# A planned three-stage kernel whose order now comes from backward plans, with stores of y and of hi parts issued by ScalarE

## The chip, the cores and the metric

The kernel runs on one core of a Trainium2 chip, in one launch. The metric is device time in microseconds (us), the median of several runs. The engines are named as in the profile: PE is TensorE's matmul unit and PEld its weight load, DVE is VectorE, ACT is ScalarE, POOL is GpSimd, SP is SyncE, which here does nothing but issue transfers.

## What is computed

```python
def sm_attn(qq, kk, vv):
    s = scale * np.matmul(qq, kk.transpose(0, 1, 3, 2))
    s = s - np.max(s, axis=-1, keepdims=True)
    a = np.exp(s)
    a = a / (np.sum(a, axis=-1, keepdims=True) + 1e-09)
    return np.matmul(a, vv)
p_packed = sm_attn(p, k, v)               # 8 batches, 8 heads, 576 tokens, 32 packed, 64 wide
out = sm_attn(q, p_packed, p_packed)
...
h = x @ w_in                              # x: out as 4608 tokens x 512; w_in: 512 x 1024
sm = softmax(h); solu = h * sm
ln = (solu - mean(solu)) / sqrt(var(solu) + 1e-06) * g_ln
x = ln @ w_out                            # 1024 x 512
...
g = relu(x @ moe2_w_in) ** 2              # 512 x 2048
return g @ moe2_w_out                     # 2048 x 512
```

The weights come as 64-bit floats, which the kernel turns into 32-bit ones itself. Data is 32-bit; most products are made as three products of hi and lo parts (hi*hi, hi*lo, lo*hi).

## The kernel before

The program has three stages that flow into each other. In the first, 16 units (a batch and four of its heads) are packed (`pack`: scores `s1`, their exponentials `e1`, transposes `pt`, the product `ppp` with the rows of v, and its transpose `ptp`, which becomes `ppq`) and unpacked (`unpack`: scores `s2` of q, a softmax over the 32 packed rows, its transposition to `aT`, and the product `pg` of the packed rows with w_in, kept as `G`). A group of 128 tokens (`h_tile`) makes h as `ph` from `G` and the split parts `ah`, `al` of `aT`, goes through softmax and layer norm to `e`, and is transposed (`ptv`) and split into `v`. For 256 tokens `y_stage` makes y = v times w_out in four banks `py` of 24 products each; ACT copies a bank to `ysb`, and a transfer stores it to `y_dram`. Beside it, 16 pieces of moe2's first matrix are decoded from 64-bit floats (`prepare`), summed for a Strassen-like scheme of 7 products, split into hi (`wh`) and lo (`wx`) and stored to `z_dram`. The second stage (`z_group`, tiles `px`, `pw`, `pz` from `y` and `zi`) makes g and stores it to `g_dram`; 16 pieces of moe2's second matrix are prepared beside it and stored to `o_dram`. The third (`o_products`, tiles `px`, `pa` from `oi` and `cb`) makes the output from g, which is loaded as `ga` and split into `cb`.

Nothing is written in the order in which it runs. Each piece of work is handed to a planner as an operation of one engine (`Plan.op`) or of one of several (`Plan.either`), with an estimated duration, the buffers that it reads and writes, and an **urgency**: a number in us, made by hand-set constants (`att_at`, `T0`, `DT`, `PD`, `WD`, `YB` and others). `Plan.order` (line 148) plays the operations forward through its own estimates; whenever an engine is free it takes the able operation of the lowest urgency, and a shared buffer goes to the lowest urgency that asks for it. The sequence in which operations start is the program's order: each engine, and each queue of transfers, runs its own operations in that order and waits at the head for what the head needs. All transfers of before but 18 of the last output stores are issued by SP (line 373, `dma`), so a store whose data is late holds the loads behind it.

```python
def dma(at, out_, in_, nbytes, r=(), w=(), spare=0, queue=nc.sync):
    plan.op(DMA, max(430.0, nbytes / 358.0), at, lambda: queue.dma_start(out=out_(), in_=in_()), r=r, w=w, lag=2200 + spare)
```

Eight PSUM banks serve PE: in the first stage four of them (`bank`, one shared ring) take turns for `s1`, `pt`, `ppp`, `ptp`, `s2`, `pg`, `ptv` and `py`, and two `ph` tiles hold two each. The lines that matter below: 404 to 406 (the three products of `mm`), 386 and 389 (hi and lo of a split), 478 and 560 (scores), 648 (`pg`), 696 and 719 (`ph`), 762 (`ptv`), 785 (`ysb`), 438 (the last addition of a decoded weight), 733 and 750 (passes over `e`).

Of the kernel before, what the change touches and what calls it, by code (L numbers as in the profile page):

```python
# [9 lines left out]
F32 = mybir.dt.float32  # L10
# [9 lines left out]
PE, ACT, DVE, POOL, DMA = range(5)  # L20
# [70 lines left out]
class Plan:  # L91

    WINDOW = 3413.0

# [22 lines left out]
    def either(self, engines, urgency, fn, r=(), w=(), lag=0, claim=(), port=False):  # L120
# [25 lines left out]
        self.ops.append(Op(engines, urgency, fn, lag, bufs, deps, port))  # L146

    def order(self):
        ops = self.ops
        users = [[] for _ in ops]  # L150
# [29 lines left out]
        order = []  # L180
# [11 lines left out]
        def take(e, t):  # L192
            nonlocal port
            while not busy[e] and able[e]:
                _, i = heapq.heappop(able[e])
                o = ops[i]
                if o.engine is not None:
                    continue
                o.engine = e
                busy[e] = True  # L200
                order.append(i)
                if e == POOL or e == DVE and o.port:
                    port = self.span = max(t, port) + o.engines[e]
                else:
                    self.span = pe_end(t, o.engines[e]) if e == PE else t + o.engines[e]
                heapq.heappush(events, (self.span, i, "free"))
# [29 lines left out]

    def emit(self):
        with self.tc.manual_schedule():
            for i in self.order():
# [6 lines left out]
def kernel(  # L246
# [25 lines left out]
    nc = tc.nc  # L272
# [5 lines left out]
    P = 128  # L278
# [4 lines left out]
    KJ = (S + P - 1) // P  # L283
    SH = S // 2
    ST = 256
    AB, GB, RAW, TMP, VR, ET = 4, 4, 1, 2, 1, 1
    QA, GA, HA, TR, UN = 55.91, 149.84, 34.68, -39.93, -11.33
    NK = 4
    WD, WDS, WIS = 99.51, 175.52, 17.0
    GSC = (POOL,)  # L290
    SIN, SOUT = DVE, ACT
    GX = 1
    SUB, KLO, ALO = (POOL,), (DVE,), (DVE,)
    ZSIN, OSIN = DVE, DVE
    SN, FN, LATE = 5.72, -26.79, 3090.0
    YB, ZL, OL, GL0, GL1, GL2, PS, CS = 197.3, 148.71, 20.73, 15.29, 13.31, 32.6, 1.04, 186.23
    NST = NT // ST
# [39 lines left out]
    y_dram = [dram.tile([P, CD, 2 * HN], F32, name=f"y_dram{i}", tag=f"y{i}") for i in range(NSZ)]  # L337
# [32 lines left out]

    def dma(at, out_, in_, nbytes, r=(), w=(), spare=0, queue=nc.sync):

        plan.op(DMA, max(430.0, nbytes / 358.0), at, lambda: queue.dma_start(out=out_(), in_=in_()), r=r, w=w, lag=2200 + spare)
# [98 lines left out]
    pbz = [ab.tile([P, 2, HG, 32] if i == 0 else [P, 2, 2, 32], F32, f"pbz{i}") for i in range(3)]  # L472
    PAIR = 4 * (0.4336 * SH + 6)

# [17 lines left out]
    def pack(at, b, g):  # L492
# [105 lines left out]
        def pp_mm():  # L598
            for j in range(KJ):
                m = rows[j]  # L600
                for e in range(2):
                    nc.tensor.matmul(
                        ppp()[64 * e:64 * e + 64, :2 * D].rearrange("p (h m i) -> p h m i", h=2, m=2),
                        eT()[:m, j, 64 * e:64 * e + 64], vr()[:m, 2 * e:2 * e + 2, j, :].rearrange("p m (h i) -> p h m i", h=2), start=j == 0, stop=j == KJ - 1)
        plan.op(PE, KJ * 267, at + 10, pp_mm, r=[eT, vr], w=[ppp])

# [20 lines left out]
    def unpack(at, b, g, packed):  # L627
# [13 lines left out]
        for f in range(F1 // 512):  # L641
            pg = bank("pg")
            fs = slice(f * 512, (f + 1) * 512)

            def g_mm(pg=pg, fs=fs):
                for e in range(2):
                    es = slice(64 * e, 64 * e + 64)
                    nc.tensor.matmul(pg()[es, :], ppq()[:, e], wi[2 * g + e]()[:, fs], start=True, stop=True)  # L648
            plan.op(PE, 885, at + GA, g_mm, r=[ppq, wi[2 * g], wi[2 * g + 1]], w=[pg], claim=[gt])
            hi_op(at + GA + 1, 512, lambda fs=fs: gt()[:, 0, fs], pg, [pg], [gt])  # L650
            if b >= GX:
                lo_op(at + GA + 1, 512, lambda fs=fs: gt()[:, 1, fs], pg, lambda fs=fs: gt()[:, 0, fs], [pg, gt], [gt], (DVE,))
# [116 lines left out]
    def y_stage(at, st):  # L769
        vh, vl = v_tiles.pop(st)  # L770
        t, o = divmod(st * ST, 2 * HN)
        for d in range(CD):
# [8 lines left out]
            for half in range(2):  # L781
# [4 lines left out]
                    r=[py], w=[ysb] + [under_way] * (st == d == 0))  # L786
            dma(at - YB, lambda d=d: y_dram[t][:, d, o:o + ST], ysb, P * ST * 4, r=[ysb], w=[ydep[t]])

# [5 lines left out]
    def prepare(at, w_bits, rows2, cols2, outs, marks, tiles, sign, r=(), engines=BOTH, spare=0):  # L794
# [11 lines left out]
        lo_op(at, 7 * P, lambda: x().bitcast(F32R), x, hi, [hi], [x], engines)  # L806
        dma(at, outs[0], lambda: hi().bitcast(F32), P * 7 * P * 4, r=[hi], w=marks)
        dma(at, outs[1], x, P * 7 * P * 4, r=[x], w=marks)
# [7 lines left out]

    T0, DT = 127.57, 23.948
    PD0, PD = 111.2, 23.139
    UD, UA, U1 = 25.541, 213.28, -45.68
    WI, WO, WOD, YL = 162.35, 266.68, 65.988, 3.36  # L820
    units = [(b, g) for b in range(B) for g in range(NG)]
# [31 lines left out]
    ORDER = (1, 2, 6, 5, 7, 3, 4)  # L853
    DZ, DO = 5.018, 7.511
    T1 = T0 + DT * NT / P
# [302 lines left out]
    second()  # L1158
    plan.emit()

# [29 lines left out]
```

## Time and profile before

| what | value |
|---|---|
| median of 3 runs (lowest, highest) | 1265.01 us (1264.72, 1267.79) |
| the profiled execution | 1262.49 us, of which 1260.4 us are its span |
| PE busy | 1205.5 us, 96% of the span, 8332 products |
| DVE, ACT, POOL busy | 906.0, 789.7, 171.7 us |
| mean granted TensorE clock | 0.985 |
| transfers | 234.60 MB, mean 186 GB/s |

How to read it: busy PE is time in which at least one product is under way, and the ends of products are modelled, so the span between two starts tells more than a duration. The span starts with the first instruction and ends with the last; the execution's own time has 2.1 us around it.

### The profile page before, as it was taken

The numbers are of one execution on the slowest core, as the hardware profiler recorded it, in microseconds if no ns is written. First come the engines' busy times: TensorE is split into PE (matmuls) and PEld (weight loads), VectorE is DVE, ScalarE is ACT, GpSimd is POOL, SyncE is SP. The second block draws the span as 40 slices with busy tenths as digits, with TensorE's granted clock in tenths as the row PEclk, the third lists the DMA queues.
The fourth block names the chain that finished last, engine by engine and source line by source line (L and its number), as shares of the span: only waits on it lengthen the run. The fifth ranks groups of instructions, "written<-read, shape, count | busy, mean of one in ns | idle before, by whom it ended". The sixth has DMA issues, their size and how long they took to land.

```text
span 1260.4 us, 23326 instructions
## 1 busy us (share of the span) xinstructions
PE 1205.5 (96%) x8332; PEld 1101.2 (87%) x8332; DVE 906.0 (72%) x1817; ACT 789.7 (63%) x1678; POOL 171.7 (14%) x181
## 2 busy tenths in 40 slices
PE   4668999999999999999999999999899999999998
PEld 2336788877888789999999999999899999999998
DVE  5888678787766874455686868662678787878786
ACT  2476577666776666577777878777554555555453
POOL 1364323333332340000000000000000000000000
PEclk9878999999999999999999999999899999999999
DMA  8856756776756649465767676753986535343501
GB/s 214 224 154 168 204 156 174 216 197 170 205 150 193 171 125 329 157 200 197 242 199 248 205 249 206 230 166 130 351 341 210 157 121 158 112 151 110 171 32 51
DMA packets 185240, 234.60 MB, mean 186 GB/s; under 512 B 24356, under 2 KB 148772, under 8 KB 184356
## 3 DMA queue, kind: packets, MB, share of 16 engines
q1 hardware_dynamic: 184260, 232.33, 60.2%
q8 instruction: 65, 1.06, 0.4%
q10 hardware_dynamic: 864, 0.79, 0.2%
q14 instruction: 51, 0.42, 0.1%
HBM read 130.55 MB, written 85.98 MB: 172 GB/s over the span
## 4 chain that ended last, share of the span: by engine, by line
PE 78%; DMA 5%; DVE 4%; ACT 3%; issue 1%; SPq 1%; ACTq 0%; DVEq 0%
PE px L404 9%; PE px L406 8%; PE px L405 8%; PE ph L719 7%; PE py L404 5%; PE py L405 5%; PE py L406 5%; PE pa L404 5%; PE pa L406 5%; PE pa L405 5%; PE ptv L762 3%; PE s L478 2%; PE pg L648 2%; PE pz L406 2%; PE pz L405 2%; PE pz L404 2%
## 5 line engine op out<-in xcount | busy, mean ns | idle before, releaser
L386 ACT CAST cb<-ga 128x384 fp32r<-128x384 f32 x336 | 168.0, 513 | 168.3 <-PE px L406 70.9
L389 DVE TENSOR_TENSOR cb<-ga,cb 128x384 fp32r<-128x384 f32 x336 | 180.5, 555 | 60.8 <-ACT cb L386 59.5
L404 PE MATMUL py<-v,wo 128*128 128x256 f32 x576 | 169.3, 294 | 0.0
L405 PE MATMUL py<-v,wo 128*128 128x256 f32 x576 | 163.5, 284 | 0.0
L406 PE MATMUL py<-v,wo 128*128 128x256 f32 x576 | 163.2, 283 | 0.0
L404 PE MATMUL px<-oi,cb 128*128 128x256 f32 x504 | 142.8, 283 | 2.9 <-ACT cb L386 2.9
L406 PE MATMUL px<-oi,cb 128*128 128x256 f32 x504 | 142.5, 283 | 0.8 <-DVE cb L389 0.8
L405 PE MATMUL px<-oi,cb 128*128 128x256 f32 x504 | 142.4, 282 | 0.0
L404 PE MATMUL pa<-oi,cb 128*128 128x256 f32 x504 | 141.4, 281 | 0.0
L406 PE MATMUL pa<-oi,cb 128*128 128x256 f32 x504 | 141.0, 280 | 0.0
L405 PE MATMUL pa<-oi,cb 128*128 128x256 f32 x504 | 141.0, 280 | 0.0
L404 PE MATMUL px<-y,zi 128*128 128x384 f32 x384 | 130.3, 339 | 1.8 <-ACT gw L963 1.7
L405 PE MATMUL px<-y,zi 128*128 128x384 f32 x384 | 129.6, 337 | 0.4 <-DVE y L389 0.3
L406 PE MATMUL px<-y,zi 128*128 128x384 f32 x384 | 129.3, 337 | 0.0
L404 PEld LDWEIGHTS py<-v,wo 128*128 128x128 f32 x576 | 110.6, 192 | 9.1 <-issue 7.8
L967 DVE TENSOR_TENSOR gw<-pz,gw 128x384 f32<-128x384 f32 x96 | 53.2, 554 | 81.1 <-PE pz L406 66.2
L405 PEld LDWEIGHTS py<-v,wo 128*128 128x128 f32 x576 | 110.8, 192 | 0.7
L406 PEld LDWEIGHTS py<-v,wo 128*128 128x128 f32 x576 | 110.6, 192 | 0.0
L907 DVE TENSOR_TENSOR ga<-ga 128x384 f32<-128x384 f32 x192 | 99.7, 552 | 2.6 <-DMA ga<-g_dram 1.9
L404 PEld LDWEIGHTS px<-oi,cb 128*128 128x128 f32 x504 | 96.4, 191 | 3.2 <-ACT cb L386 3.2
L406 PEld LDWEIGHTS px<-oi,cb 128*128 128x128 f32 x504 | 96.5, 191 | 1.1 <-DVE cb L389 1.1
L975 ACT ACTIVATE gw<-gw 128x384 f32<-128x384 f32 x115 | 60.2, 523 | 57.5 <-DVE gw L967 57.1
(180 smaller groups left out, 2990.8 us busy)
## 6 DMA issues: line engine op xcount, KB each, us to landing
g_dram<-gw SPq DMA_DIRECT2D x192, 192.0 KB
ga<-g_dram SPq DMA_DIRECT2D x96, 384.0 KB
zi<-z_dram SPq DMA_DIRECT2D x28, 512.0 KB
oi<-o_dram SPq DMA_DIRECT2D x24, 512.0 KB
kr<-in_k_dram SPq DMA_DIRECT2D x16, 576.0 KB
qr<-in_q_dram SPq DMA_DIRECT2D x16, 576.0 KB
q<-qT SPq DMA_DIRECT2D x64, 144.0 KB
y_dram<-ysb SPq DMA_DIRECT2D x72, 128.0 KB
```

What stands on the lines that cost most here:

```text
L386: plan.op(ACT, c_act(cols, sbuf=r[0].pool not in (psm, psh, pso)), at, lambda: nc.scalar.copy(out_(), in_()), r=r, w=w)
L389: plan.either(on(cols, *engines), at, lambda e: vec[e].tensor_tensor(out_(), in_(), hi_().bitcast(F32), op=ALU.subtract), r=r, w=w, port=i ...
L404: nc.tensor.matmul(ps, lh, rh, start=first, stop=False, skip_group_check=onto)
L405: nc.tensor.matmul(ps, lh, rl, start=False, stop=False, skip_group_check=onto)
L406: nc.tensor.matmul(ps, ll, rh, start=False, stop=last, skip_group_check=onto)
L478: nc.tensor.matmul(ps()[64 * e:64 * e + 64, :SH], cols(lhs, e), cols(rhs, e)[:, cs], start=True, stop=True)
L648: nc.tensor.matmul(pg()[es, :], ppq()[:, e], wi[2 * g + e]()[:, fs], start=True, stop=True)
L719: nc.tensor.matmul(ph()[:, fs], al[l]()[:, g], g_tiles[b, g]()[:, r, fs], start=ends[0] and g == 0 and t == 0, stop=ends[1] and g == NG - ...
L762: nc.tensor.transpose(pt()[:, c * P:(c + 1) * P], e()[:, (4 * t + c) * P:(4 * t + c + 1) * P], ident)
L907: plan.op(DVE, c_dve(cols), at, lambda: nc.vector.tensor_tensor(out_(), in0(), in1(), op=op), r=r, w=w, port=True)
L967: plan.op(DVE, c_dve(HN), when(p, SN), lambda: nc.vector.tensor_tensor(t(), ps()[:, :HN], t(), op=ALU.add), r=[t, ps], w=[t])
L975: nc.scalar.activation(t(), t(), AF.Relu)
```

## The change

Three things are changed. First, the order is no longer planned once. `emit` plans forward as before, then eight times (`PASSES`) plans the same operations backward from the end, with the engines and buffer slots that the forward plan chose, and takes each operation's distance from the end of the backward plan as its new urgency before it plans forward again. The hand-set constants only feed the first plan; several have new values. Second, the planner's estimates differ: every transfer lands 1500 ns later (`spare=1500` by default), and `s1`/`s2`, `ppp` and `pg` last a little longer. Third, 72 stores of y, 16 of `z_dram`'s hi part and 16 of `o_dram`'s hi part are issued from ACT's queue (`queue=nc.scalar`), and the subtraction that makes `al` belongs to POOL instead of DVE (`ALO`). No product is added or removed: PE has the same 7962 instructions in another order. Lines of the changed kernel carry numbers 65 higher.

```diff
+    def reset(self):
+        for o in self.ops:
+            o.engine = None
+            for b in o.bufs:
+                b.slot = None
+                if b.ring:
+                    b.ring.free, b.ring.queue = list(range(b.ring.bufs)), []
+
+    def backward(self):
+
+        ops, ends = self.ops, self.ends
+        deps = [set(o.deps) for o in ops]
+        slots = {}
+        for b in dict.fromkeys(b for o in ops for b in o.bufs if b.slot is not None):
+            slots.setdefault((b.ring, b.slot), []).append(b)
+        for bufs in slots.values():
+            bufs.sort(key=lambda b: ends[b.touched[0]])
+            for a, b in zip(bufs, bufs[1:]):
+                deps[b.touched[0]].update(a.touched)
...
+                for j in sorted(deps[i]):
+                    left[j] -= 1
+                    free[j] = max(free[j], t + self.hop(ops[j].engine, e) + ops[j].lag)
+                    if not left[j]:
+                        heapq.heappush(events, (free[j], j, "ready"))
+            for e in (PE, ACT, POOL, DVE, DMA):
+                if not busy[e] and able[e]:
+                    _, i = heapq.heappop(able[e])
+                    busy[e] = True
+                    starts[i] = now + ops[i].engines[e]
...
+        end = max(starts)
+        for o, t in zip(ops, starts):
+            o.urgency = round((end - t) / 1e3, 6)
...
-    def emit(self):
+    def emit(self, passes):
+        order = self.order()
+        for _ in range(passes):
+            self.backward()
+            order = self.order()
...
-    SUB, KLO, ALO = (POOL,), (DVE,), (DVE,)
+    PASSES = 8
+    SUB, KLO, ALO = (POOL,), (DVE,), (POOL,)
...
-    def dma(at, out_, in_, nbytes, r=(), w=(), spare=0, queue=nc.sync):
+    def dma(at, out_, in_, nbytes, r=(), w=(), spare=1500, queue=nc.sync):
...
-    PAIR = 4 * (0.4336 * SH + 6)
+    PAIR = 4 * (0.4336 * SH + 6) + 85
...
-        plan.op(PE, KJ * 267, at + 10, pp_mm, r=[eT, vr], w=[ppp])
+        plan.op(PE, KJ * 280 + 60, at + 10, pp_mm, r=[eT, vr], w=[ppp])
...
-            plan.op(PE, 885, at + GA, g_mm, r=[ppq, wi[2 * g], wi[2 * g + 1]], w=[pg], claim=[gt])
+            plan.op(PE, 957, at + GA, g_mm, r=[ppq, wi[2 * g], wi[2 * g + 1]], w=[pg], claim=[gt])
...
-            dma(at - YB, lambda d=d: y_dram[t][:, d, o:o + ST], ysb, P * ST * 4, r=[ysb], w=[ydep[t]])
+            dma(at - YB, lambda d=d: y_dram[t][:, d, o:o + ST], ysb, P * ST * 4, r=[ysb], w=[ydep[t]], queue=nc.scalar)
...
-        dma(at, outs[0], lambda: hi().bitcast(F32), P * 7 * P * 4, r=[hi], w=marks)
+        dma(at, outs[0], lambda: hi().bitcast(F32), P * 7 * P * 4, r=[hi], w=marks, queue=nc.scalar)
...
-    T0, DT = 127.57, 23.948
-    PD0, PD = 111.2, 23.139
+    T0, DT = 119.98, 22.429
+    PD0, PD = 133.89, 25.885
...
-    plan.emit()
+    plan.emit(PASSES)
```

The first place where the order matters below is PE's queue around the first y product, which needs v of 256 tokens. Before, these rows stand there (`pg` is unit 3's, numbers are of buffers):

```order
L762 MATMUL ptv_777<-ident_60,e_569 128x128 x4
L648 MATMUL pg_784<-wi2_325,ppq_750 64x512
L648 MATMUL pg_784<-wi3_379,ppq_750 64x512
L648 MATMUL pg_800<-wi2_325,ppq_750 64x512
L648 MATMUL pg_800<-wi3_379,ppq_750 64x512
L404 MATMUL py_814<-v0_726,wo000_533 128x256
L405 MATMUL py_814<-v1_747,wo000_533 128x256
```

and now:

```order
L827 MATMUL ptv_788<-ident_60,e_659 128x128 x4
L784 MATMUL ph_797<-G_309,ah_146 128x512 x2
L784 MATMUL ph_797<-G_457,ah_146 128x512 x2
L543 MATMUL s1_820<-k2_718,pbz1_752 64x288 x2
L543 MATMUL s1_831<-k2_718,pbz1_752 64x288 x2
L469 MATMUL py_837<-v0_754,wo000_519 128x256
L470 MATMUL py_837<-v1_765,wo000_519 128x256
```

The scores `s1` of the fifth unit (8 products: each row stands for two and their pairs) and 4 products of `ph` for the third pair of token groups now stand ahead of the first y product.

The second place is PE's queue behind it, where those scores stood before, after 36 products of y:

```order
L406 MATMUL py_856<-v0_726,wo110_632 128x256
L478 MATMUL s1_876<-k2_742,pbz1_752 64x288 x2
L478 MATMUL s1_884<-k2_742,pbz1_752 64x288 x2
L404 MATMUL py_856<-v0_726,wo101_630 128x256
L405 MATMUL py_856<-v1_747,wo101_630 128x256
```

and the first interruption of y's products now, after 48 of them:

```order
L471 MATMUL py_884<-v0_754,wo111_601 128x256
L653 MATMUL pt_929<-ident_60,e1_881 128x128 x3
L469 MATMUL py_935<-v0_754,wo20_691 128x256
L470 MATMUL py_935<-v1_765,wo20_691 128x256
L471 MATMUL py_935<-v0_754,wo21_697 128x256
```

The scores have gone from here; transposes of the exponentials that they led to stand here instead.

The third place is ACT's queue where y's first banks are copied. Before:

```order
L785 COPY ysb_874<-py_814 128x256
L386 CAST wo30_881<-wx_651 128x1024
L386 CAST ah_150<-aT_906 128x64
L750 ACTIVATE e_788<-e_788,nb_914,rst_904 128x1024
L575 ACTIVATE e1_934,sm_935<-s1_876,nmx_916 128x288
```

and now:

```order
L850 COPY ysb_903<-py_837 128x256
L438 DMA y_dram0_91<-ysb_903 128x256
L815 ACTIVATE e_804<-e_804,nb_917,rst_901 128x1024
L850 COPY ysb_933<-py_884 128x256
L451 COPY eT_951<-pt_929 128x384
L451 CAST ah_148<-aT_948 128x64
L451 CAST ah_823<-aT_948 128x128
L438 DMA y_dram0_91<-ysb_933 128x256
```

A store stands on ACT's own queue now, here once right behind its copy and once three operations later. Of the 104 stores, 27 stand right behind what makes their data, 77 have at least one other ACT operation between; 79 also wait for an earlier transfer on one of the eight shared DMA semaphores.

The fourth place is ACT's queue where the second stage ends and the third begins; the second step of the third stage needs `cb_10185` before, `cb_10182` now. Before:

```order
L386 CAST cb_10159<-ga_10127 128x384
L386 CAST cb_10169<-ga_10108 128x384
L994 ACTIVATE gw_10172<-px_10034 128x384
L976 ACTIVATE gw_10172<-gw_10172 128x384
L975 ACTIVATE gw_10097<-gw_10097 128x384
L976 ACTIVATE gw_10097<-gw_10097 128x384
L386 CAST cb_10185<-ga_10051 128x384
```

and now:

```order
L1059 ACTIVATE gw_10153<-px_10020 128x384
L451 CAST cb_10155<-ga_10098 128x384
L451 CAST cb_10174<-ga_10108 128x384
L1040 ACTIVATE gw_10082<-gw_10082 128x384
L1041 ACTIVATE gw_10082<-gw_10082 128x384
L451 CAST cb_10182<-ga_10037 128x384
```

The same casts of later tiles and the same closing passes over g stand ahead of the cast that PE needs; one pass less follows the casts.

## Rows read from the trace of the kernel before

**Rows 1.** Busy time of each engine by stage, granted clock, DMA share, GB/s.

```profile
core 0: us, PE busy (x) PEld busy (x) DVE busy (x) ACT busy (x) POOL busy (x), PEclk, DMA share, GB/s
0.00:50.00 50.00, 23.01 (x96) 12.85 (x97) 31.63 (x59) 13.10 (x30) 9.49 (x25) 0.90 0.94 225
50.00:103.00 53.00, 37.91 (x157) 18.74 (x155) 49.16 (x76) 38.54 (x66) 28.67 (x18) 0.84 0.56 158
103.00:120.00 17.00, 14.50 (x103) 13.06 (x100) 12.38 (x25) 10.14 (x23) 8.95 (x7) 0.90 0.62 172
120.00:540.00 420.00, 419.04 (x2972) 349.41 (x2971) 300.88 (x614) 276.28 (x607) 124.60 (x132) 1.00 0.65 188
540.00:880.00 340.00, 337.86 (x1919) 334.75 (x1919) 213.89 (x421) 259.79 (x548) 0.00 (x0) 1.00 0.64 209
880.00:900.00 20.00, 16.37 (x93) 15.76 (x92) 10.23 (x20) 11.93 (x25) 0.00 (x0) 0.91 0.90 299
900.00:1240.00 340.00, 340.00 (x2861) 340.00 (x2861) 279.22 (x587) 176.84 (x376) 0.00 (x0) 0.99 0.49 161
```

**Rows 2.** PE's timeline around the first y product: start, duration, idle before and releaser.

```profile
88.98 0.69 PE L588 MATMUL pt<-ident,e 128*128 128x128 f32 x2 [7.05 <-ACT e L575]
...
103.41 0.39 PE L404 MATMUL py<-v,wo 128*128 128x256 f32 x1
...
110.42 1.30 PE L478 MATMUL s<-k,pbz 128*64 128x288 f32 x8 [2.28 <-DVE G L389]
111.64 0.58 PE L404 MATMUL py<-v,wo 128*128 128x256 f32 x1
...
115.10 0.28 PE L405 MATMUL py<-v,wo 128*128 128x256 f32 x1
...
117.25 0.28 PE L405 MATMUL py<-v,wo 128*128 128x256 f32 x1
```

**Rows 3.** The chain that ended last, one piece of it: six ph products at full clock.

```profile
153.03 1.40 PE ph L719 x6
```

**Rows 4.** ACT's timeline: the second token group's e is finished.

```profile
80.55 1.24 ACT L750 ACTIVATE e<-e,nb,rst 128x1024 f32<-128x1024 f32 x1 [1.60 <-DVE nb L748]
```

**Rows 5.** DVE's and POOL's timelines in the first 110 us.

```profile
43.03 2.06 DVE L438 TENSOR_TENSOR wi<-wi,wraw 128x1024 f32<-128x1024 f32 x1
...
107.88 1.21 DVE L733 SCALAR_TENSOR_TENSOR e<-ph,e 128x1024 f32<-128x1024 f32 x1
...
94.29 1.90 DVE L389 TENSOR_TENSOR al<-aT,ah 128x64 fp32r<-128x64 f32 x1
...
93.76 2.35 POOL L389 TENSOR_TENSOR wo<-wx,wo 128x1024 fp32r<-128x1024 f32 x1 [1.16 <-ACT wo L386]
```

**Rows 6.** All of one operation: al; ysb; wh; stores on ACT: min/median/max ns.

```profile
L389 DVE TENSOR_TENSOR al<-aT,ah x70: 209/282/2090, 94.3 to 496.6; 128x128 fp32r<-128x128 f32 x56, 128x64 fp32r<-128x64 f32 x14
...
L785 ACT COPY ysb<-py x72: 348/372/403, 110.3 to 578.8; 128x256 f32<-128x256 f32 x72
...
L386 ACT CAST wh<-wx x32: 923/934/951, 126.5 to 813.7; 128x896 fp32r<-128x896 f32 x32
...
L373 ACTq DMA_DIRECT2D out_dram<-osb x18: 321/376/440, 1242.8 to 1257.8; - x18
```

**Rows 7.** SP's queue, whom it waited for: us in total, times, longest.

```profile
SPq L373 <- ACT ysb L785: 95.0, 37, 9.7
...
SPq L373 <- DMA oi<-o_dram: 16.7, 16, 2.4
```

**Rows 8.** PE's waits, one row of them.

```profile
PE px L404 <- ACT gw L963: 1.7, 5, 0.6
```

**Rows 9.** PE's and ACT's timelines where the second stage ends.

```profile
896.42 0.46 PE L404 MATMUL px<-oi,cb 128*128 128x256 f32 x1 [2.87 <-ACT cb L386]
...
892.81 0.93 ACT L386 CAST cb<-ga 128x384 fp32r<-128x384 f32 x2 [1.90 <-DMA ga<-g_dram]
...
893.64 0.48 ACT L994 ACTIVATE gw<-px 128x384 f32<-128x384 f32 x1
```

More of the change, by code (lines that the diff above doesn't have):

```diff
@@ L146, in either @@
         self.ops.append(Op(engines, urgency, fn, lag, bufs, deps, port))
+    def reset(self):
[15 more added lines that the diff above has]
+                deps[b.touched[0]].update(a.touched)
+        left = [0] * len(ops)
+        for i, d in enumerate(deps):
+            d.discard(i)
+            for j in d:
+                left[j] += 1
+        able = [[] for _ in range(5)]
+        busy = [False] * 5
+        free, starts = [0.0] * len(ops), [0.0] * len(ops)
+        port = 0.0
+        events = [(0.0, i, "ready") for i in range(len(ops)) if not left[i]]
+        heapq.heapify(events)
+        while events:
+            now = events[0][0]
+            while events and events[0][0] <= now:
+                t, i, what = heapq.heappop(events)
+                e = ops[i].engine
+                if what == "ready":
+                    heapq.heappush(able[e], (-ends[i], i))
+                    continue
+                busy[e] = False
+                for j in sorted(deps[i]):
[8 more added lines that the diff above has]
+                    starts[i] = now + ops[i].engines[e]
+                    if e == POOL or e == DVE and ops[i].port:
+                        port = starts[i] = max(now, port) + ops[i].engines[e]
+                    heapq.heappush(events, (starts[i], i, "free"))
+        end = max(starts)
+        for o, t in zip(ops, starts):
+            o.urgency = round((end - t) / 1e3, 6)
@@ L148, in order @@
     def order(self):
         ops = self.ops
+        self.reset()
+        self.ends = [0.0] * len(ops)
         users = [[] for _ in ops]
@@ L205, in take @@
                     self.span = pe_end(t, o.engines[e]) if e == PE else t + o.engines[e]
+                self.ends[i] = self.span
                 heapq.heappush(events, (self.span, i, "free"))
@@ L235, in order @@
         return order
-    def emit(self):
+    def emit(self, passes):
[3 more added lines that the diff above has]
+            order = self.order()
         with self.tc.manual_schedule():
-            for i in self.order():
+            for i in order:
                 self.ops[i].fn(self.ops[i].engine)
@@ L286 @@
     AB, GB, RAW, TMP, VR, ET = 4, 4, 1, 2, 1, 1
-    QA, GA, HA, TR, UN = 55.91, 149.84, 34.68, -39.93, -11.33
+    QA, GA, HA, TR, UN = 15.37, 149.84, 60.66, -52.41, -15.5
     NK = 4
-    WD, WDS, WIS = 99.51, 175.52, 17.0
+    WD, WDS, WIS = 101.7, 198.675, 19.564
     GSC = (POOL,)
@@ L292 @@
     GX = 1
-    SUB, KLO, ALO = (POOL,), (DVE,), (DVE,)
+    PASSES = 8
+    SUB, KLO, ALO = (POOL,), (DVE,), (POOL,)
     ZSIN, OSIN = DVE, DVE
-    SN, FN, LATE = 5.72, -26.79, 3090.0
-    YB, ZL, OL, GL0, GL1, GL2, PS, CS = 197.3, 148.71, 20.73, 15.29, 13.31, 32.6, 1.04, 186.23
+    SN, FN, LATE = 56.95, -26.79, 3090.0
+    YB, ZL, OL, GL0, GL1, GL2, PS, CS = 189.17, 148.71, 22.45, 15.29, 2.98, 32.6, 1.04, 186.23
     NST = NT // ST
@@ L814 @@
     g_mark = [[[plan.mark("g") for _ in range(4)] for b in range(4)] for st in range(NSZ)]
-    T0, DT = 127.57, 23.948
-    PD0, PD = 111.2, 23.139
+    T0, DT = 119.98, 22.429
+    PD0, PD = 133.89, 25.885
     UD, UA, U1 = 25.541, 213.28, -45.68
-    WI, WO, WOD, YL = 162.35, 266.68, 65.988, 3.36
+    WI, WO, WOD, YL = 162.35, 269.12, 65.988, 3.39
     units = [(b, g) for b in range(B) for g in range(NG)]
@@ L853 @@
     ORDER = (1, 2, 6, 5, 7, 3, 4)
-    DZ, DO = 5.018, 7.511
+    DZ, DO = 4.851, 7.511
     T1 = T0 + DT * NT / P
```

## The prediction

> **What bounds the kernel now.** I read the stages first, because a share of the whole span mixes different limits. In the table of stages [rows 1] the reader is to see three things. From 120 us on PE is all but full: 419.04 of 420 us, 337.86 of 340 and 340.00 of 340, so nothing that only speeds up another engine can pay there. In the first 50 us PE works 23.01, DVE 31.63, and the transfers are at 0.94 of what the 16 DMA engines can carry: bytes set the pace. From 50 to 103 us DVE is busy 49.16 of 53 us and PE 37.91: DVE sets the pace. So PE has only about 42 us of idle time ahead of 103 us (27.0 and 15.1), 2.5 us from 103 to 120, and 3.6 us near 880. Everything to be won lies there.
>
> Next I read PE's timeline around the first product of y [rows 2], since from that product on PE can be kept full. It starts at 103.41 us. Before it PE stood 7.05 us (until 88.98) for an exponential; behind it PE stood 2.28 us for a bank that DVE had to empty (`G`), and after that stop it ran slowly: the 16 products from 111.64 to 115.10 take 0.216 us each, the 18 from 115.10 to 117.25 take 0.119. The stages show a mean granted clock of 0.90 for 103 to 120 us, and of 1.00 behind it; 0.119 is the pace of the upper level (2.4 GHz), and the slow pace follows the stop.
>
> **The change, part by part.** The sum is made against the profiled execution, 1262.49 us (2.1 us of it around the span); the median, 1265.01, lies 2.5 us above, and I add that at the end.
>
> Term 1: work moved ahead of the first y product. Four `ph` products go there, 0.233 us each by the six in 1.40 us [rows 3], together 0.93; and the eight scores of the fifth unit, which took 1.22 us from their start to the next product's [rows 2]. If they fill time in which PE stands anyway, 2.15 us of work is gone from behind the first y product, where PE is full. I take -2.0, between 0 (the first y product moves back by as much) and -2.2.
>
> Term 2: the stretch behind the first y product. The scores that stopped y's products are gone from there. With them goes the idle 2.28 us, and the slow pace behind it, which cost 3.46 - 16 x 0.119 = 1.55 us. The next interruption now comes after 48 products instead of 36, that is 1.4 us later, and needs exponentials whose scores are long done. I take -3.8. The other end: a stop of the same 2.28 us for the transposes on top of what stands there now, +2.3.
>
> Term 3: the time of the first y product itself. It hangs on DVE's queue. One addition of a decoded w_in, 2.06 us, leaves that queue for POOL, one pass over `e`, 1.21 us, comes into it [rows 5], and the `al` of early groups leave it. That is 0.85 us less, but the addition lies at 43 us, in the stretch where DVE idles 18.4 of 50 us while bytes set the pace, so it moves nothing; the 7.05 us wait stands in front of an exponential that DVE feeds. The `ptv` behind that wait needs an `e` that ACT had ready at 80.55 + 1.24 = 81.8 us [rows 4], 7 us before PE got to it, yet v comes after more DVE work, which is full. I take 0, between -3.8 (all that DVE idles from 50 to 103 us is won) and +4.2 (two of the `al` on POOL come 2.09 us late each, the longest one by [rows 6]).
>
> At this term a rule is weighed. The row first: an `al` of 128x64 took 1.90 us on DVE beside a POOL operation of 2.35 us that had begun half a microsecond earlier [rows 5], while the median `al` takes 0.282 [rows 6]. The Trainium skill, SBUF — State Buffer, section "Who interferes with whom", says that a DVE operation with two SBUF inputs and a GpSimd operation that reads SBUF lock each other out for a whole instruction, whoever starts first winning. By that rule `al` on POOL does not leave DVE alone but can hold its two-input operations, which speaks against this part of the change. The trace agrees with it in those 1.90 us. If each of two early `al` held DVE for 0.45 us, an estimate, the sum would come out 0.9 us higher.
>
> Term 4: steady work from 120 to 880 us. ACT gets 104 stores. An issue takes 0.376 us by the only stores that ACT issues now [rows 6], so 104 x 0.376 = 39 us; the 27 that stand directly behind their producer also wait for it to land, about as long again as a `ysb` copy (0.372) or, at worst, as a `wh` (0.934): 10 to 25 us. ACT is idle 143.7 us from 120 to 540 and 80.2 us from 540 to 880 [rows 1]; that is the cover, and some 50 to 64 us of 224 fit in it. What is queued behind a waiting store on ACT are the passes over `e`, the `ysb` copies and, in the second stage, `gw`; for `gw` PE waits 0.34 us a time, five times [rows 8]. If the cover is gone, that is the price. SP in turn is freed: it stood 95.0 us for `ysb`, once 9.7 us [rows 7], with loads behind it. But the loads that PE needs were not late: SP's waits for `oi` come to 16.7 us, and PE's own idle time in the two stages is 0.96 + 2.14 us [rows 1]. The 70 `al` add at 0.282 us some 20 us to POOL, which has 295 idle from 120 to 540. I take 0, between -3.1 (PE's idle time of both stages) and +9.2 (27 stores at 0.34).
>
> Term 5: from the second stage to the third. PE stood 2.87 us for `cb`; ACT's cast had waited 1.90 us for the load of `ga` [rows 9]. In the new order the same casts and closing passes stand ahead, with one pass less (0.48 us) behind them. The load sets it, and every load is now planned 1.5 us later, so it is issued no later. I take 0, between -2.9 and +2.
>
> Sum: -2.0 - 3.8 = -5.8 on 1262.49 gives 1256.7; with the 2.5 us of the median, 1259.2. I forecast **1259 us**.
>
> **The rivals.** No change: the start is bound by bytes and by DVE, not by PE's order. PE then only waits elsewhere: the scores moved ahead push the first y product back, and the stop that is gone behind it comes back at the transposes. For it: DMA share 0.94 and DVE 49.16 of 53 us. Against it: the stop of 2.28 us belonged to one order of two banks and nothing in DVE's total asks for it. Terms 1 and 2 then shrink to some -0.5: 1264.5 us. That the stores in another queue bring nothing belongs to it: SP's 95.0 us hid behind a full PE. The Trainium skill, DMA: Bandwidth & Descriptors, section "Issuing engines are not separate DMA queues", says that transfers of all issuing engines share the same 16 DMA engines, and that another issuer saves only the issue time; no run here shows it yet.
>
> Slower: ACT stands for semaphores. 79 of the 104 stores also wait for an earlier transfer on one of eight shared semaphores, and on ACT that wait stops all else. Place: 120 to 880 us. If half of them wait as long as SP's longest for `oi`, 2.4 us, ACT stands 40 x 2.4 = 96 us more; it decides once ACT's work and waits pass nine tenths of a stage, which 259.8 of its work, 30 of those waits and 20 of issues, 310 of 340 us, reach from 540 to 880. Where PE then waits for `gw` at 0.34 us, 40 times, that is +13.6: 1272.8 us. Against it: these stores were planned 1.5 us late, so most earlier transfers should have landed.
>
> Faster by more: the 7.05 us wait goes. In the new order `ptv` need not stand behind the transposes of a late exponential, and y starts earlier by as much: 1259.2 - 7.05 = 1252.1 us. For it: `e` was ready 7 us before. Against it: DVE must split v for that, and DVE is full.
>
> **How the numbers follow.** Chances: the forecast 0.42 (its own range 1254 to 1264), no change 0.23, slower 0.16, faster by more 0.19. The range goes from 1246 (faster by more, and PE's idle time of terms 4 and 5 gone too: 1252.1 - 3.1 - 2.9) to 1272, which leaves out half of the slower case and little at the other end. A measurement can tell 0.3%, 3.8 us, from no change: faster means below 1261.2, slower above 1268.8. Below fall 0.34 of the forecast's 0.42, all 0.19 and 0.02 of the no-change case: 0.55. Above fall 0.14 of the slower case and 0.03 of the others: 0.17. The rest is 0.28.
>
> **What would show it.** Right: in the changed profile the first y product starts at 99 to 107 us, the scores before it, with no idle time over 1 us in the 48 products behind it and a granted clock near 1.00 from there to 120 us. ACT's own queue issues 122 transfers, with PE's busy time from 120 to 880 us still above 99%. Wrong: a first y product over 4 us earlier or later (term 3), stops at the transposes (term 2), PE waiting often for `ysb` or `gw` because ACT stands at a store (term 4), or a stop at the third stage's start other than 1 to 5 us (term 5).

## The result, and the profile after

The changed kernel takes 1253.29 us (median of 3 runs, 1252.65 to 1254.32) against 1265.01 us: 11.7 us less, a ratio of 0.9913 with a 95% interval of 0.9888 to 0.9938. The two profiled executions are 1253.29 and 1262.49 us, 9.2 us apart; the other 2.5 us are the distance of the profiled execution of before from its own median. So the traces explain 9.2 us.

The stages of the changed kernel answer to [rows 1]; the columns are the same.

```profile
0.00:50.00 50.00, 24.74 (x92) 13.08 (x92) 31.58 (x53) 12.71 (x29) 11.38 (x26) 0.97 0.86 199
50.00:103.00 53.00, 37.03 (x165) 18.08 (x166) 50.97 (x82) 38.09 (x67) 31.95 (x19) 0.94 0.70 198
103.00:120.00 17.00, 16.66 (x126) 14.35 (x124) 10.83 (x23) 11.56 (x25) 9.18 (x10) 1.00 0.42 124
120.00:540.00 420.00, 417.19 (x2956) 346.78 (x2957) 286.93 (x550) 275.65 (x606) 152.85 (x196) 1.00 0.65 189
540.00:880.00 340.00, 340.00 (x1941) 339.98 (x1940) 217.79 (x430) 260.72 (x545) 0.00 (x0) 1.00 0.66 212
880.00:900.00 20.00, 17.87 (x120) 17.46 (x120) 15.77 (x34) 11.96 (x27) 0.00 (x0) 0.91 1.02 386
900.00:1240.00 340.00, 340.00 (x2875) 340.00 (x2875) 278.14 (x587) 174.66 (x374) 0.00 (x0) 1.00 0.47 152
```

Read it from the third line. From 103 to 120 us PE's busy time rises from 14.50 to 16.66 us and its clock from 0.90 to 1.00. From 120 to 540 it *falls*, by 1.85 us. From 540 to 880 it is 340.00 of 340, where 2.14 us had been idle. ACT's busy time is where it was (275.65 and 260.72, against 276.28 and 259.79), with 104 stores more in its queue.

Busy time hides slow products, so one more measure is worked out from the traces. PE's products fall into small groups (the four of a transposition, two of `ph`, one of `y`). A group's price is the time from its start to the next group's, at the 20th percentile of its kind, the lowest that any of the fourteen profiles of this study shows. All prices add up to some 1138 us; whatever a stretch takes beyond the prices of its groups, with the time before the first product, is **lost time**. The time from the start of the last product to the end of the span (3.8 us before, 4.2 now) is in no column:

```
us lost            to 120  120-540  540-880  880-920  after   span
before               68.0     30.9      8.9      7.2    3.7  1260.4
changed              62.4     33.7      4.6      4.5    3.7  1251.4
```

Three places gain (5.6, 4.3 and 2.7 us) and one loses (2.8 us). That makes 9.8 us where the spans differ by 9.0, so the table is good to about 1 us: with the products grouped in another way the start gains 4.9 us and the stretch from 120 to 540 loses 3.1, while the columns from 540 to 920 stay as they are.

For the gain of 4.3 us from 540 to 880 one row of before names what is gone. PE's weight loads waited there for g's first pass (`gw`), and in the changed kernel no such wait is left in that stretch (us, times, longest):

```profile
PEld px L404 <- ACT gw L963: 4.3, 8, 0.9
```

The start, in PE's timeline (columns as in [rows 2]):

```profile
101.08 3.70 PE L784 MATMUL ph<-G,ah 128*128 128x512 f32 x8 [0.43 <-ACT ph L802]
104.72 1.19 PE L543 MATMUL s<-k,pbz 128*64 128x288 f32 x8
105.84 0.39 PE L469 MATMUL py<-v,wo 128*128 128x256 f32 x1
...
111.58 0.28 PE L471 MATMUL py<-v,wo 128*128 128x256 f32 x1
111.70 0.49 PE L653 MATMUL pt<-ident,e 128*128 128x128 f32 x3
111.94 0.36 PE L469 MATMUL py<-v,wo 128*128 128x256 f32 x1
```

The first y product comes at 105.84 us, 2.43 later than before, but 3.64 + 1.12 = 4.8 us of other work (each from its start to the next start) is done ahead of it. Behind it 48 products run at 0.12 us each without a stop, and the transposes slip in without one: the 2.28 us stop and the slow products of [rows 2] are gone.

The end of the second stage, PE's and ACT's timelines, answers to [rows 9]:

```profile
888.86 0.39 PE L469 MATMUL px<-oi,cb 128*128 128x256 f32 x1 [2.04 <-ACT cb L451]
...
888.31 1.32 ACT L451 CAST cb<-ga 128x384 fp32r<-128x384 f32 x3
```

The stop is 2.04 us, and no wait of ACT for the load of `ga` stands ahead of it. SP's timeline tells why. First before:

```profile
881.46 0.32 SPq L373 DMA_DIRECT2D ga<-g_dram  x1
883.53 0.38 SPq L373 DMA_DIRECT2D ga<-g_dram  x1
886.77 1.12 SPq L373 DMA_DIRECT2D ga<-g_dram  x2
890.43 0.90 SPq L373 DMA_DIRECT2D ga<-g_dram  x2
```

then the changed kernel:

```profile
873.67 0.32 SPq L438 DMA_DIRECT2D ga<-g_dram  x1
875.26 0.38 SPq L438 DMA_DIRECT2D ga<-g_dram  x1
878.50 2.89 SPq L438 DMA_DIRECT2D ga<-g_dram  x4
882.60 0.37 SPq L438 DMA_DIRECT2D ga<-g_dram  x1
```

PE stops at 896.42 - 2.87 = 893.55 before and at 888.86 - 2.04 = 886.82 now. Five us ahead of that stop SP had issued four loads of `ga` before, and has issued six now.

### The profile page after: what moved, and what is told of

Same layout as the page of the kernel before. It is cut to its first block, busy times and chain, and to the rows that moved or that the text cites. A ratio compares the mean times of both kernels' runs of the same rounds, so it can differ in the third digit from the quotient of the medians.

```text
span 1251.4 us, 23307 instructions
## 1 busy us (share of the span) xinstructions
PE 1201.0 (96%) x8332; PEld 1097.0 (88%) x8332; DVE 894.0 (71%) x1756; ACT 785.4 (63%) x1669; POOL 205.3 (16%) x250
## 4 chain that ended last, share of the span: by engine, by line
PE 84%; DMA 7%; DVE 4%; POOL 2%; ACT 1%; issue 1%; SPq 1%; DVEq 0%; POOLq 0%; ACTq 0%
PE px L469 10%; PE px L471 10%; PE px L470 10%; PE ph L784 7%; PE pa L469 5%; PE pa L471 5%; PE pa L470 5%; PE py L469 4%; PE py L470 4%; PE py L471 4%; PE pz L470 3%; PE pz L471 3%; PE pz L469 3%; PE ptv L827 2%; PE s L543 2%; PE pg L713 2%
## 5 line engine op out<-in xcount | busy, mean ns | idle before, releaser
L469 PEld LDWEIGHTS px<-oi,cb 128*128 128x128 f32 x504 | 95.9, 190 | 2.2 <-ACT cb L451 2.2
L471 PEld LDWEIGHTS px<-oi,cb 128*128 128x128 f32 x504 | 96.0, 190 | 0.3 <-DVE cb L454 0.3
L470 PEld LDWEIGHTS px<-oi,cb 128*128 128x128 f32 x504 | 95.6, 190 | 0.0
```

The costliest lines, as they stand in the source:

```text
L469: nc.tensor.matmul(ps, lh, rh, start=first, stop=False, skip_group_check=onto)
L470: nc.tensor.matmul(ps, lh, rl, start=False, stop=False, skip_group_check=onto)
L471: nc.tensor.matmul(ps, ll, rh, start=False, stop=last, skip_group_check=onto)
```

## The experiments

Twelve kernels ran, in three groups of four. Each group has its own runs of the kernel before, with medians of 1264.61, 1265.16 and 1267.18 us, so compare ratios, not times, between groups. Where a difference of two ratios is given in us, it is taken of 1265 us. The changed kernel has only the three runs of its own; e1 is the run nearest to it, with the same order on PE.

```
                                              us   ratio   95% interval
changed                                  1253.29  0.9913  0.9888-0.9938
e1  changed, stores on SP                1255.68  0.9922  0.9900-0.9945
e2  changed, al on DVE, planned anew     1263.37  0.9996  0.9983-1.0010
e3  changed, no backward pass            1286.02  1.0170  1.0149-1.0191
e4  changed, no late landing             1278.06  1.0119  1.0093-1.0146
e5  before + passes                      1264.84  0.9996  0.9983-1.0008
e6  before + passes + late landing       1272.12  1.0055  1.0034-1.0076
e7  before + stores on ACT               1267.51  1.0024  1.0012-1.0037
e8  changed, seven passes                1261.09  0.9962  0.9946-0.9978
e9  changed, al on DVE in place          1259.44  0.9941  0.9923-0.9959
e10 new start, old rest                  1270.54  1.0029  1.0015-1.0043
e11 old start, new rest                  1261.30  0.9953  0.9936-0.9970
e12 start of e5, new rest                1253.68  0.9897  0.9879-0.9916
```

Their lost time, by the measure above:

```
us lost   to 120  120-540  540-880  880-920  after   span
e1          62.6     38.0      4.6      4.6    3.6  1255.4
e2          65.1     40.6      6.5      3.1    3.7  1260.8
e3          75.6     41.5      8.2      6.0   11.2  1284.1
e4          65.1     50.4     10.3      2.7    3.9  1275.7
e5          58.6     41.7     11.8      3.0    3.9  1262.4
e6          62.2     51.5      4.7      4.4    3.7  1268.1
e7          67.4     34.5     10.6      7.3    3.8  1265.2
e8          62.6     40.9      5.5      4.5    3.7  1259.2
e9          65.1     37.5      5.2      3.1    3.7  1257.1
e10         63.0     41.3     10.2      8.1    2.3  1266.9
e11         69.1     34.8      5.3      3.1    3.7  1257.7
e12         60.2     37.0      4.7      3.0    3.7  1250.9
```

Each row is one execution. Two pairs run the same order on PE and differ in the stores' queue alone: changed and e1, before and e7. They lie within 0.6 us of each other to 120 and from 880 on and within 1.7 us from 540 to 880, but 4.3 and 3.6 us apart from 120 to 540. So a difference of some 4 us in that column, the changed kernel's 2.8 against before among them, says little about an order.

### The stores' queue: e1 and e7

e1 takes `queue=nc.scalar` out of the changed kernel; e7 puts it into the kernel before. In both, every compute engine's order stays as it was.

```diff
-            dma(at - YB, lambda d=d: y_dram[t][:, d, o:o + ST], ysb, P * ST * 4, r=[ysb], w=[ydep[t]], queue=nc.scalar)
+            dma(at - YB, lambda d=d: y_dram[t][:, d, o:o + ST], ysb, P * ST * 4, r=[ysb], w=[ydep[t]])
...
-        dma(at, outs[0], lambda: hi().bitcast(F32), P * 7 * P * 4, r=[hi], w=marks, queue=nc.scalar)
+        dma(at, outs[0], lambda: hi().bitcast(F32), P * 7 * P * 4, r=[hi], w=marks)
```

> The changed kernel with its 104 stores issued by SP again; every engine's order is the same but for them. If the gain of 11.7 us is the order of PE's work in the first 120 us (where PE lost 8 us less), this stays at 1251 to 1256 us, because SP's waits for ysb lie behind a full PE. If the stores' queue is what brought the gain (loads no longer held behind late data), it goes back to 1260 to 1266 us, with PE idle for loads from 120 to 540 us.

> The kernel before in its own order, with only the 104 stores issued by ACT. If SP's 95.0 us of waits for ysb hide behind a full PE: 1261 to 1268 us. If the stores' queue pays in every order: 1255 to 1260 us. If ACT stands for its stores: over 1270 us, with PE waiting for ysb, G or gw.

With the stores on SP the changed kernel measures 0.9922 instead of 0.9913, which can't be told apart. SP's queue in e1 (whom it waited for: us, times, longest) shows that the waits for `ysb` are all back:

```profile
SPq L438 <- ACT ysb L850: 100.6, 43, 9.1
```

They hold nothing that PE needs soon: from 540 to 880 us PE is full in e1 too, and the 4.3 us that its one profile loses more from 120 to 540 shrink to 1.1 us by the ratios. (Its expectation speaks of 8 us lost less in the first 120 us; by the table it is 5.6.) In the old order the stores on ACT make the kernel 0.24% slower, about 3 us, with an interval that excludes no change. So the queue alone is not where the gain is. The Trainium skill, DMA: Bandwidth & Descriptors, section "Issuing engines are not separate DMA queues", has it that another issuer saves only the issue time; by that rule little was to be had, and both runs agree.

### Passes and late landing: e3 to e6

e3 sets `PASSES = 0`, e4 sets `spare=0`, each with the rest of the change kept. e5 adds `reset`, `backward` and eight passes to the kernel before, with its constants, estimates, queues and `al`; e6 is e5 with `spare=1500`.

```diff
-    PASSES = 8
+    PASSES = 0
```

```diff
-    def dma(at, out_, in_, nbytes, r=(), w=(), spare=1500, queue=nc.sync):
+    def dma(at, out_, in_, nbytes, r=(), w=(), spare=0, queue=nc.sync):
```

> The changed kernel with no backward pass: urgencies from the hand-set constants in their new values, with late landing, ACT's stores and al on POOL kept. If urgencies from backward plans bring the gain, this loses all of it or more: 1262 to 1272 us, the loss in the first 120 us and near 880. If constants, landing time or queues brought it: 1251 to 1256 us.

> The changed kernel with transfers that land as estimated (no extra 1500 ns); backward passes, queues and al kept. If late landing is what matters (transfers planned too tightly make engines wait): 1259 to 1266 us, with waits of PE for loads and a longer stop where the third stage starts. If the backward plans alone bring the gain: 1251 to 1256 us.

> The kernel before with its own constants, landing times, queues and al, and only the eight backward passes added. If backward plans need late landing beside them (each load is placed just in time by its estimate, and ACT then stands for it as it stood 5.39 us for w2raw in the run without the extra 1500 ns): slower than before, 1268 to 1285 us. If passes help by themselves: 1251 to 1258 us.

> As the run before this one, with transfers that land 1500 ns later in the plan; constants, queues and al are those of before. If passes with late landing are the whole of the gain, whatever the constants: 1251 to 1258 us. If the new constants, or the choice of one order among many like it, matter as much: 1260 to 1272 us, and under the run with passes alone.

In the changed kernel each is worth far more than the whole gain: without passes some 33 us are lost, without late landing 26, both beyond every range that I had named. The places were not all as expected either. e3 loses 13 us more than the changed kernel to 120 us, but also 8 from 120 to 540 and 7.5 behind 920; e4 loses 17 from 120 to 540, and its stop where the third stage starts is not longer (2.7 us lost against 4.5). e3's timeline of PE shows two stops in the start, for a load and for an exponential:

```profile
101.73 2.38 PE L543 MATMUL s<-k,pbz 128*64 128x288 f32 x8 [10.68 <-DMA k<-kT]
...
112.31 1.97 PE L827 MATMUL ptv<-ident,e 128*128 128x128 f32 x8 [6.32 <-ACT e L640]
```

In e4 one mechanism shows in the timelines of ACT and PE. A cast of a decoded weight stands at the head of ACT's queue until its load lands; the `ysb` copy behind it would empty the bank that PE needs:

```profile
289.72 0.66 ACT L484 ACTIVATE wx<-w2raw 128x512 f32<-128x512 f32 x1 [5.39 <-DMA w2raw<-in_moe_w_in_dram]
290.29 0.57 ACT L451 CAST v<-ptv 128x512 fp32r<-128x512 f32 x1
290.75 0.38 ACT L850 COPY ysb<-py 128x256 f32<-128x256 f32 x1
...
291.18 0.65 PE L827 MATMUL ptv<-ident,e 128*128 128x128 f32 x4 [3.32 <-ACT ysb L850]
```

From 120 to 900 us ACT's waits for `w2raw` come, in e4, to

```profile
ACT wx L484 <- DMA w2raw<-in_moe_w_in_dram: 22.3, 8, 5.9
```

and in the changed kernel to

```profile
ACT wx L484 <- DMA w2raw<-in_moe_w_in_dram: 4.8, 6, 1.6
```

PE's own waits for `ysb` come to 7.4 us in e4 from 120 to 540, so this accounts for under half of the 17 us lost there; the rest is spread over other waits.

But on the constants of before the same two steps bring nothing: passes alone 0.9996, passes with late landing 1.0055. My expectation that e5 would be slower missed, and so did the rival that passes help by themselves. e6 missed both of its own: it is not faster than before, and it is slower than e5 where the second had it under e5. What parts e6 from the changed kernel is the constants, the longer estimates for three kinds of product, the stores' queue and `al`; the constants and the estimates were not tried by themselves. Neither step has a worth of its own that holds in both settings.

### The scatter of one order against another: e8, e2 and e9

e8 changes only the number of passes, which plays no part in any mechanism:

```diff
-    PASSES = 8
+    PASSES = 7
```

> The changed kernel with seven backward passes instead of eight, which plays no part in any mechanism and only gives another order of the same kind; it measures the scatter from one order to another. If the gain is a property of backward plans with late landing: 1250 to 1258 us. If it is the choice of this one order: 1258 to 1270 us, and then the 10 us lost with al on DVE says nothing about al.

Seven passes measure 0.9962 where eight measure 0.9913: some 6 us, over half of the whole gain, for another order of the same kind, with intervals that do not overlap. The lost time shows where: 62.6 against 62.4 us to 120, but 40.9 against 33.7 from 120 to 540. That is the control for every run that plans anew, e2 among them.

```diff
-    SUB, KLO, ALO = (POOL,), (DVE,), (POOL,)
+    SUB, KLO, ALO = (POOL,), (DVE,), (DVE,)
```

> The changed kernel with the subtraction that makes al on DVE again; eight backward passes, so the whole order is planned anew. If moving al is worth nothing: 1251 to 1257 us, the rest being scatter of one order against another. If relief of DVE brought the gain: 1259 to 1266 us. If POOL's al holds DVE's operations with two SBUF inputs, DVE's time per such operation falls and the kernel is faster: 1246 to 1250 us.

By itself e2 (0.9996) would say that `al` on POOL is worth nearly all of the gain. e9 asks the same with the order frozen. The list of operations stays as the changed kernel planned it, and only the engine of the 70 subtractions is changed before they are issued:

```diff
+    def mix(self, order):
+        for o in self.ops:
+            if o.engine == POOL and o.bufs[-1].name.startswith("al"):
+                o.engine = DVE
+        return order
...
-        with self.tc.manual_schedule():
+        order = self.mix(order)
+        self.place(order)
+        with self.tc.manual_schedule():
```

(`place` gives out the shared banks again along the list, in e9 to e12; what that alone does to the time was not measured.)

> The changed kernel's order kept operation by operation; only the 70 subtractions that make al are issued by DVE instead of POOL, at the same places in the order, with no planning anew. If al on POOL is worth little and the 10 us lost with al on DVE came from another order: 1251 to 1257 us. If relief of DVE is worth it: 1259 to 1265 us.

0.9941 against 0.9913: some 3.5 us, with intervals that overlap, and much less than e2's ten. The median of 1259.44 us is at the foot of the second expectation, but this group's kernel before is 2 us slower than the others'; by its ratio e9 lies between the two. Whether relief of DVE pays anything stays open. All of `al` in the changed kernel (min/median/max ns):

```profile
L454 POOL TENSOR_TENSOR al<-aT,ah x70: 312/461/861, 94.3 to 489.6; 128x128 fp32r<-128x128 f32 x56, 128x64 fp32r<-128x64 f32 x14
```

and in e9:

```profile
L481 DVE TENSOR_TENSOR al<-aT,ah x70: 182/282/1494, 96.9 to 497.1; 128x128 fp32r<-128x128 f32 x56, 128x64 fp32r<-128x64 f32 x14
```

POOL's is slower in the median but has no long outlier.

### Start and rest apart, with frozen orders: e10 to e12

These kernels plan nothing anew. A table holds the order and engines of another plan of the same 5557 operations, and the list is stitched: the first 820 operations of one plan, then the others in the order of the second plan. After 820 operations the plans of before and of the change have started the same ones but for five. The stores are on ACT in all three, so e7 is the partner with old start and old rest.

```diff
+    def mix(self, order):
+        raw = zlib.decompress(base64.b85decode(OLD))
+        n = len(order)
+        old, engines = struct.unpack(f"<{n}H", raw[:2 * n]), raw[2 * n:]
+        head = order[:820]
+        early = set(head)
+        for i, (o, e) in enumerate(zip(self.ops, engines)):
+            if i not in early:
+                o.engine = e
+        return head + [i for i in old if i not in early]
```

e11 takes `old[:820]` as the head and `order` behind it; in e12 the table holds e5's plan and 540 of its operations are the head.

> The first 820 of the plan's 5557 operations (to about 190 us) in the changed kernel's order, all others in the order of the kernel before, nothing planned anew (at that point the two plans have started the same operations but for five); 104 stores on ACT. Measured against the kernel before with stores on ACT (1267.5 us). If the gain of the start is its own and carries to the end: 1261 to 1265 us, that is 3 to 6 us off. If the rest of the order gives it back: 1266 to 1269 us.

> The mirror of the run before this one: the first 820 operations in the order of the kernel before, all others in the changed kernel's. If the gain is half the start's and half that of the second stage and its end: 1256 to 1260 us. If it is the start's alone: 1262 to 1266 us. If it is the rest's alone: 1251 to 1255 us.

> The first 540 operations (to about 125 us) in the order of the run that added only the backward passes to the kernel before, where PE had done 4.1 us more work by 120 us than in the changed kernel; the others in the changed kernel's order, nothing planned anew. If what the start gains carries to the end: 1247 to 1251 us, faster than both kernels. If later stages give it back: 1252 to 1257 us.

The four corners are 1.0024 (both old, e7), 1.0029 (new start alone), 0.9953 (new rest alone) and 0.9913 (both new). The new rest alone is worth 0.7%, some 9 us against e7; the new start brings nothing on the old rest and, on the new one, 0.4%, some 5 us, with intervals that just touch. Stages of e7 (columns as in [rows 1]):

```profile
0.00:120.00 120.00, 77.44 (x357) 45.19 (x359) 94.65 (x159) 62.09 (x118) 47.14 (x49) 0.80 0.73 189
120.00:360.00 240.00, 238.15 (x1679) 192.04 (x1676) 181.00 (x371) 158.49 (x350) 82.89 (x87) 1.00 0.66 184
```

and of e10:

```profile
0.00:120.00 120.00, 80.41 (x375) 46.18 (x376) 92.64 (x154) 62.34 (x119) 52.70 (x54) 0.84 0.74 188
120.00:360.00 240.00, 232.23 (x1637) 187.44 (x1636) 176.08 (x356) 154.38 (x346) 85.89 (x98) 0.99 0.66 183
```

The new start does put PE ahead, by 2.97 us of busy time (4.4 us of lost time). Then the old rest loses 5.92 us of it to 360. Most of what PE waits for there is DVE's, as if DVE's part of the next units had not come along; no run tests that. PE's waits of e10 from 120 to 240 us begin with

```profile
PE ptp L851 <- DVE pp L841: 3.3, 2, 2.5
PE ptv L995 <- ACT e L983: 1.0, 2, 0.5
```

while no wait of PE in e7 comes to more than 0.5 us in that stretch. e12 says the same more mildly: its start is 2.2 us better than the changed kernel's, and it loses 3.3 us more from 120 to 540. It has the lowest ratio of all, 0.9897, but is not told apart from the changed kernel's 0.9913. By the ratios e10 and e12 came out where the start is given back, and e11 (0.9953, 1259 us) where the gain is half the start's and half the rest's.

### What the fourteen profiles say together

Three stretches split cleanly by the two parts of the change. From 540 to 880 us all profiles whose order there comes from passes with late landing lose 4.6 to 6.5 us, and all others 8.2 to 11.8. Passes alone don't do it (e4, e5), nor does late landing alone (e3). In e5 the old wait of [rows 8] is still there:

```profile
PE px L469 <- ACT gw L1028: 3.5, 4, 1.3
```

From 880 to 920 us passes are enough: 2.7 to 4.6 us with them, 6.0 to 8.1 without. To 120 us passes give 58.6 to 65.1, hand-set urgencies 67.4 to 75.6. The fourth stretch goes the other way. From 120 to 540 us before loses 30.9 us, and whole plans made with passes lose 33.7 to 51.5; the changed kernel is the lowest of these, though e1 with the same order on PE lost 38.0. That stretch decides which of them is faster than before. Why this one order does so well there was not found out.

## Why the prediction was right or wrong

The forecast was 1259 us, and 1253.29 lies inside the range 1246 to 1272 and on the side that had most of the chance. It lies just below the forecast's own range of 1254 to 1264.

**Terms 1 to 3, the start: the sum right, two entries wrong.** I had -2.0, -3.8 and 0, that is -5.8; the traces show 68.0 - 62.4 = 5.6 us less lost. Term 1 was priced by the wrong row. The four `ph` products are those of the first batch, which are not split into hi and lo, and they took 3.64 us to the next start instead of 0.93 (the profile has two records for each of them). A row of before for two of them was in the chain that ended last:

```profile
126.42 1.91 PE ph L719 x4
```

So 4.8 us went ahead of the first y product, not 2.15; and term 3, which I took as 0, was +2.4, inside its bounds. The two errors cancel, which is luck. Term 2's stop and slow pace did go as named; what is left of the 5.6 us is about 5.6 - (4.8 - 2.4) = 3.2 us against 3.8 (2.5 if the start gained 4.9).

**Term 4, steady work: 0 is not what happened.** It is +2.8 us from 120 to 540, within what two executions of one order on PE differ by, and -4.3 from 540 to 880. The cover that I named for the stores held: ACT's busy time is unchanged and e1 and e7 bound the stores within some 3 us. What I missed is that the waits for `gw` from 540 to 880 were there to be won. I read them in PE's row alone [rows 8], 1.7 us; in the weight loads' row, shown above, they come to 4.3 us, as much as the stretch gained. PE's idle time stood in my bound, -3.1, not in the value.

**Term 5: 0 was taken, -2.7 came.** I wrote that the load sets the stop and that a load planned to land later is issued no later, and stopped there. It is issued earlier against the end of the stage, six loads instead of four, and ACT's 1.90 us wait of [rows 9] is gone. The runs put it down to the passes (e4, without late landing, loses 2.7 us there).

So the executions differ by 9.2 us where 5.8 were forecast, and terms 4 and 5 (2.8 - 4.3 - 2.7 = -4.2 us, where I had 0) cover the 3.4 us between, within the 1 us of the table: the step that failed is the value 0 for both, where their waits stood in rows. The other 2.5 us of the miss come from adding the distance between the profiled execution and the median of before, which the changed kernel's profiled execution does not have.

**The rivals.** No change lost its main argument: the start did gain although DVE was full. e10 shows what was right in it, since the start's lead is given back unless the rest can use it. The slower rival (ACT standing for semaphores) did not come in the changed kernel; in e7 the stores cost 3 us. But its place was well chosen: in e4 ACT stands, for loads and not for stores, and the kernel is 13 us slower than before by the group's medians. The faster rival gave 1252.1 us, nearest of all, by a mechanism that did not happen: the first y product comes later, not 7.05 us earlier.

**The views named for it** came out as listed for right: first y product at 105.84, 48 products without a stop, clock 1.00 from 103 to 120 us, PE 99.6% busy from 120 to 880 (757.19 of 760), a stop of 2.04 us. ACT issues 72 + 32 + 18 = 122 transfers.

On the rule about DVE and GpSimd: the holding shows in the traces, at a small price. `nb`, a DVE operation on two inputs of 128x1, takes 0.159 us (median) in the 27 cases in which POOL is idle, and never over 0.160. Beside an `al` that POOL had begun 0.01 us earlier it took 0.46 us and ended with it:

```profile
416.87 0.46 DVE L813 SCALAR_TENSOR_TENSOR nb<-nmu,rst 128x1 f32<-128x1 f32 x1 [0.66 <-POOL rst L811]
...
416.86 0.46 POOL L454 TENSOR_TENSOR al<-aT,ah 128x128 fp32r<-128x128 f32 x1
```

That is what the Trainium skill, SBUF — State Buffer, section "Who interferes with whom", says of a DVE operation with two SBUF inputs. Counted over the changed kernel, `al` on POOL lengthened eight DVE operations by over 0.1 us, 1.7 us in all, the first of them at 136.74 us; so the 0.9 us that I set against two early `al` did not come. On DVE in e9, `al` was itself lengthened seven times by POOL's other operations, 4.2 us in all. The rule is there, then, but it does not speak against this part of the change.

## What to carry to other kernels

Where a planner makes the order, measure first what a change without meaning does to it: one pass less cost some 6 us here, so a run that plans anew tells nothing about an edit worth 3 us. Freeze the order and edit in place, or stitch two orders, to give each part its own price. A lead that PE gains in one stage counts only as far as the engines that feed the next stage come along, and a product must be priced by the row of its own kind.

## What was not expected of the hardware

The mean granted clock of a stretch is only as good as its records. The changed kernel and e1 run the same order on PE. To 50 us the stages give the one a clock of 0.97, as shown above, and the other 0.80:

```profile
0.00:50.00 50.00, 22.77 (x92) 12.23 (x92) 30.98 (x52) 12.80 (x29) 11.40 (x26) 0.80 0.87 196
50.00:103.00 53.00, 40.43 (x162) 19.96 (x163) 48.61 (x81) 37.89 (x66) 30.20 (x19) 0.81 0.71 201
```

But the changed kernel's trace has no record of the clock ahead of 36.0 us, and e1's none ahead of 14.2 (before's first is at 29.6); a stretch without a record counts as 1.00. The products tell the pace. The eight scores near 30 us take 2.26 us in both kernels, and eight of the same kind 1.26 near 55 us, so near 30 us PE ran at the pace of the lower level (1.2 GHz) in both. The changed kernel's rows:

```profile
29.73 2.26 PE L543 MATMUL s<-q,ppq 128*64 128x288 f32 x8 [0.36 <-ACT ppq L451]
...
54.99 1.26 PE L543 MATMUL s<-q,ppq 128*64 128x288 f32 x8 [0.92 <-ACT ppq L451]
```

From 50 to 103 us both have records, 0.94 and 0.81, and e1's PE is busy 3.4 us longer with nearly the same products. Its first y product comes 1.2 us later (107.00 against 105.84), and to 120 us the two have lost 62.6 and 62.4 us: where PE waits for DVE and the transfers anyway, most of what slower products cost goes into waits.
